# The small constant in the denominators of an attention block: added by ScalarE instead of by two matrix products of TensorE

## The chip, the cores and the metric

The kernel runs on one core of a Trainium2 chip. The metric is the device time of one execution in microseconds (us). A core has five engines that run their own instruction streams and wait for each other through semaphores: TensorE (PE in the profile, with PEld for its weight loads), VectorE (DVE), ScalarE (ACT), GpSimd (POOL) and SyncE (SP), which here only issues DMA transfers. Matrix products go into eight banks of PSUM; everything else lies in SBUF.

## The reference

Two blocks follow each other. The first is a kernelized attention over 4 batches, 4 heads, 1088 positions and head size 32. The second routes the 4352 rows that come out of it over 8 experts with Sinkhorn weights. Cut to what matters here:

```python
def phi(x):                       # 8 x 8 = 64 features of one position
    a = einsum('rd,bhsd->bhsr', S1, x)
    b = einsum('rd,bhsd->bhsr', S2, x)
    return einsum('bhsi,bhsj->bhsij', a, b).reshape(..., 64)

q_p, k_p = phi(q), phi(k)
kv  = einsum('bhsf,bhsd->bhfd', k_p, v)
z   = sum(k_p, axis=2)
num = einsum('bhsf,bhfd->bhsd', q_p, kv)
den = einsum('bhsf,bhf->bhs', q_p, z)[..., None] + 1e-06
x   = (num / den), turned to (4352, 128)

P = exp(x @ w_gate - max), then 8 times: rows normed, columns normed
out = sum over experts e of P[:, e] * (relu(x @ w1[e]) @ w2[e])
```

The change is about one term of it: the `+ 1e-06` in `den`, for batches 1 to 3.

## The kernel before

**Stages.** Nearly all TensorE work is the expert block: the two products per expert for chunks of columns of `xT`, the attention's result with the 128 features on the partitions. Expert work needs only the columns that are done, so the kernel does batch 0's attention first (`divide`, lines 398 to 413, which adds 1e-6 with a VectorE instruction of its own) and then mixes the attention of batches 1 to 3 with expert work on the columns that exist already. After that comes the routing (Sinkhorn), mixed with expert work too, and then the main part, `weighted()` (line 1111), in which VectorE and ScalarE run along with TensorE's 64 x 64 products (lines 1158 and 1311).

**Order of the work.** The order is written out by hand at lines 1578 to 1670. `attention(b)` (line 510) is a generator: it records one step of batch `b` and yields a number, and the caller records that much expert work with `fill(n)` (line 893). An expert block is a first product into a bank (`first`, L772, 64 output rows on each half of TensorE's columns), a Relu by ScalarE that copies it out (L774), differences on VectorE (L787) and, eight steps later, the second product (L836). TensorE and VectorE keep this order; ScalarE's instructions stand where they were recorded, and each engine runs its list strictly in order.

**Banks.** `bank()` hands out one of four PSUM banks (tile name `a`) for L772's results, for the key and query projections (L306, L429), for the key sums (L336) and for `tops`. A bank is free again when its last reader is done.

**Batches 1 to 3, step by step.** A batch is done in three parts `c` of 96 positions per quarter.

- `times(b, c)` (L456): VectorE makes the query features `ph`.
- `tops(b, c)` (lines 458 to 471): TensorE multiplies `ph` (as weights, 64 columns on each column half) with `kvs`, which holds `kv` and `z` side by side: 12 instructions with 66 columns (L465). They fill `pn`, a bank that reads as 3 x 4 x 33: 32 numerators and one denominator for each of 3 position groups and 4 heads. Then two more products (L469) with 12 columns add the constant: `ones` as weights, `eps` (a tile of 1e-6/128) as data, so that the sum over 128 rows is 1e-6, into the 12 denominator columns alone.
- `over(b, c)` (lines 475 to 484): VectorE takes the reciprocal of the 12 denominators out of the bank (L478), multiplies the numerators with it (L480) and turns the result (L484).
- `take_over` (line 486) brings the turned result through DRAM to `xT` (L489, L491): by GpSimd's queue, and for the last part of batch 3 by SyncE's. The routing's first product (`logits`, L499) reads it.

An instruction with fp32 operands shows in the trace as two TensorE records, so the 108 products of L465 are 216 records and the 18 of L469 are 36.

Of the kernel before, what the change touches and what calls it, by code (L numbers as in the profile page):

```python
# [11 lines left out]
F32 = mybir.dt.float32  # L12
U32 = mybir.dt.uint32
Act = mybir.ActivationFunctionType
# [38 lines left out]
def kernel(  # L53
# [12 lines left out]
    nc = tc.nc  # L66
    P = nc.NUM_PARTITIONS
    B, H, S, D = q.shape
# [14 lines left out]
    consts = ctx.enter_context(tc.tile_pool(name="consts", bufs=1))  # L83
# [11 lines left out]
    wk = early.enter_context(tc.tile_pool(name="wk", bufs=2))  # L95

    def bank():
        return aps.tile([P, 512], F32, tag="a", name="a")
# [14 lines left out]
    ones = consts.tile([P, P], F32, name="ones")  # L113
    nc.gpsimd.memset(ones, 1.0)
    warm = [aps.tile([P, 512], F32, tag="a", name="a") for _ in range(2)]
    for _ in range(6):
        for r in range(2):
            for c in range(2):
                rows, cols = slice(64 * r, 64 * (r + 1)), slice(64 * c, 64 * (c + 1))
                nc.tensor.matmul(warm[r][cols, 0:256], ones[rows, cols], ones[rows, 0:1].to_broadcast([64, 256]),  # L120
                                 start=True, stop=True, tile_position=(64 * r, 64 * c))
# [30 lines left out]
        kvs.append(consts.tile([P, 2, 2, D + 1], F32, name=f"kvs{i}"))  # L152
        nc.vector.memset(kvs[i], 0.0)

    eps = consts.tile([P, 3, H], F32, name="eps")
    nc.vector.memset(eps, 1e-6 / P)

    v_slots = []
    for i in range(2):
        t = wk.tile([P, H + 1, NT + 1, D], F32, name=f"v{i}", bufs=1)  # L160
# [123 lines left out]
    queries = {}  # L284
# [166 lines left out]
    def third(t, c):  # L451
        return t.rearrange("p i (s c n) -> p i s c n", s=2, c=3)[:, :, :, c]
# [5 lines left out]
    def tops(b, c):  # L458

        pn = bank()[:, 0:3 * H * (D + 1)].rearrange("p (t h d) -> p t h d", t=3, h=H)  # L460
        ph = third(phs[b % 2], c)
        for t in range(3):
            for i in range(2):
                for s in range(2):
                    nc.tensor.matmul(pn[64 * s:64 * (s + 1), t, 2 * i:2 * i + 2].rearrange("p h d -> p (h d)"),  # L465
                                     ph[:, i, s, 64 * t:64 * (t + 1)], kvs[b % 2][:, i].rearrange("p h d -> p (h d)"),
                                     start=(t == 0 and i == 0), stop=False, tile_position=(0, 64 * s))
        for s in range(2):
            nc.tensor.matmul(pn[64 * s:64 * (s + 1), :, :, D], ones[:, 0:64], eps, start=False, stop=True,  # L469
                             tile_position=(0, 64 * s))  # L470
        queries[b, c] = pn

    turned = {}

    def over(b, c):
        pn = queries.pop((b, c))
        rc = wk.tile([P, 16], F32, tag="rc", name="rc")[:, 0:12].rearrange("p (t h) -> p t h", h=H)
        nc.vector.reciprocal(rc, pn[:, :, :, D])  # L478
        xs = wk.tile([P, 512], F32, tag="rd", name="rd")[:, 0:384].rearrange("p (h t d) -> p h t d", h=H, t=3)
        nc.vector.tensor_tensor(xs.rearrange("p h t d -> p t h d"), pn[:, :, :, 0:D],  # L480
                                rc.unsqueeze(3).to_broadcast([P, 3, H, D]), op=Alu.mult)
        if c == 0:
            turned[b] = wk.tile([P, H, W9], F32, tag="xt", name="xt", bufs=1)
        nc.vector.transpose(out=turned[b][:, :, 96 * c:96 * (c + 1)].rearrange("p h (t s) -> p h t s", t=3), in_=xs)  # L484
# [25 lines left out]
    def attention(b):  # L510
# [6 lines left out]
        keys_kept(b)  # L517
        times(b, 1)
        tops(b, 0)
        if b == 1:  # L520
            transpose_q(2)
        yield 1.4
        if b == 1:
            over(b, 0)
            times(b, 2)
        else:
            times(b, 2)
            over(b, 0)
        tops(b, 1)
        if b == 1:  # L530
            queries_ab(2)
            repeat_a(2)
        if follows:
            repeat_b(b + 1)
        yield 1.4
        over(b, 1)
        if b + 1 == B:
            take_over(b, 0, 192, nc.gpsimd)
        yield 1.4
        tops(b, 2)  # L540
        if follows:
            transpose_k(b + 1)
# [1162 lines left out]
```

## Time and profile before

| | us |
|---|---|
| median of three runs | 883.63 |
| the three runs | 882.86 to 883.72 |
| the profiled execution | 883.02 |
| its span, first to last instruction | 881.2 |
| TensorE busy | 875.6 (99%) |
| VectorE busy | 724.0 (82%) |
| ScalarE busy | 384.6 (44%) |
| GpSimd busy | 262.8 (30%) |

The profile page gives busy time per engine, the span in 40 slices, the DMA queues, the chain of work that ended last, and groups of instructions by source line. Matrix products are pipelined, and their ends are modelled: what a product really takes of TensorE's time is read from the distance between starts, not from the duration shown. Further views of the trace that are used below: the timeline of a stretch (start, length, engine, line, operation, tiles, number of instructions, and in brackets the idle time before and what ended it), one source line's instructions with their waits, and the busy time by stage. The granted TensorE clock is full throughout.

### The profile page before, as it was taken

What the parts mean: (1) busy time and instruction counts of PE and PEld (TensorE: products, weight loads), DVE (VectorE), ACT (ScalarE), POOL (GpSimd) and SP (SyncE); (2) the same over time, 40 slices, a digit from 0 to 9 for tenths busy, and PEclk for the clock granted to TensorE, in tenths of its full rate; (3) what the DMA queues carried; (4) which work ended last, traced back from release to release, by engine and by line L of the source; (5) the groups of instructions that cost most, each with busy time, mean ns of one, the idle gap of its engine ahead of it and who ended that gap; (6) DMA issues with size and microseconds to landing.
All of it is one profiled execution on the core that took longest, in us unless ns stands there. A gap on an engine that the chain in (4) does not pass through costs nothing.

```text
span 881.2 us, 26159 instructions
## 1 busy us (share of the span) xinstructions
PE 875.6 (99%) x10828; PEld 572.4 (65%) x10828; DVE 724.0 (82%) x982; ACT 384.6 (44%) x792; POOL 262.8 (30%) x254
## 2 busy tenths in 40 slices
PE   9999999999999999999999999999999999999998
PEld 6788656877788655555555555555555566667876
DVE  8699689978888887778887778888788888888896
ACT  3455557644444433333343333334443344444442
POOL 3131125454433313222222222221323323312431
PEclk9999999999999999999999999999999999999999
DMA  8888399886666554444435544434755557567762
GB/s 260 270 273 264 96 233 245 130 260 195 197 195 198 171 160 128 136 144 128 129 94 144 137 125 126 117 115 109 194 152 148 154 139 216 152 152 220 219 194 49
DMA packets 120887, 149.08 MB, mean 169 GB/s; under 512 B 52288, under 2 KB 79808, under 8 KB 120384
## 3 DMA queue, kind: packets, MB, share of 16 engines
q1 hardware_dynamic: 112656, 136.92, 54.4%
q0 software_dynamic: 6720, 10.19, 5.8%
q8 instruction: 86, 1.41, 0.6%
q10 hardware_dynamic: 1392, 0.28, 0.2%
q14 instruction: 33, 0.27, 0.1%
HBM read 104.86 MB, written 25.99 MB: 148 GB/s over the span
## 4 chain that ended last, share of the span: by engine, by line
PE 99%; DMA 0%; DVE 0%; issue 0%; SPq 0%; DVEq 0%
PE pair L1158 39%; PE s L1311 39%; PE a L772 9%; PE s L836 7%; PE a L336 1%; PE a L465 1%; PE a L306 0%; DMA kx<-in_k_dram 0%; PE s L1323 0%; PE s L375 0%; PE a L429 0%; PE s L395 0%; PE a L499 0%; PE a L375 0%; PE a L395 0%; PE a L612 0%
## 5 line engine op out<-in xcount | busy, mean ns | idle before, releaser
L1158 PE MATMUL pair<-xf,w1x 64*64 64x320 f32 (+3 forms) x4496 | 574.1, 466 | 0.1
L1311 PE MATMUL s<-hb,w 64*64 64x480 f32 (+3 forms) x2544 | 363.4, 466 | 0.0
L1158 PEld LDWEIGHTS pair<-xf,w1x 64*64 64x64 f32 x4496 | 251.9, 133 | 116.7 <-issue 63.5
L1174 DVE CUSTOM_DVE_ANT_0 hb<-pair,copies 128x960 f32<-128x960 f32 (+3 forms) x234 | 214.8, 918 | 101.9 <-PE pair L1158 90.0
L1311 PE MATMUL s<-hb,ws 64*64 64x480 f32 (+3 forms) x1888 | 280.7, 468 | 0.0
L1311 PEld LDWEIGHTS s<-hb,w 64*64 64x64 f32 x2544 | 150.2, 133 | 76.3 <-issue 38.6
L1311 PEld LDWEIGHTS s<-hb,ws 64*64 64x64 f32 x1888 | 113.0, 133 | 56.6 <-issue 29.3
L1071 POOL TENSOR_TENSOR xf<-xT,pb 128x960 f32<-128x960 f32 (+3 forms) x40 | 70.3, 1759 | 241.0 <-ACT turn L1364 184.3
L1079 POOL TENSOR_TENSOR xf<-xf 128x960 f32<-128x960 f32 (+3 forms) x39 | 68.1, 1745 | 222.9 <-ACT turn L1364 141.1
L1171 ACT ACTIVATE hb<-pair 128x640 f32<-128x640 f32 (+3 forms) x86 | 66.4, 773 | 150.2 <-PE pair L1158 148.4
L772 PE MATMUL a<-xT,w 128*64 128x416 f32 (+3 forms) x512 | 123.0, 465 | 0.0
L774 ACT ACTIVATE hb<-a 128x416 f32<-128x416 f32 (+3 forms) x128 | 59.5, 468 | 65.7 <-PE a L772 60.5
L1216 DVE TENSOR_TENSOR hb<-hb 128x960 f32<-128x960 f32 (+3 forms) x78 | 74.8, 959 | 7.9 <-PE pair L1158 0.9
L1364 ACT COPY turn<-s 128x1 f32<-128x1 f32 x134 | 20.9, 156 | 137.5 <-PE s L1311 137.5
L1223 DVE TENSOR_TENSOR hb<-hb 128x960 f32<-128x960 f32 (+3 forms) x78 | 72.8, 933 | 7.4
L1219 DVE TENSOR_TENSOR hb<-hb 128x960 f32<-128x960 f32 (+3 forms) x78 | 75.0, 961 | 2.4 <-ACT hb L1171 0.6
L1252 ACT COPY copies<-pair 128x960 f32<-128x960 f32 (+3 forms) x78 | 59.9, 768 | 35.5 <-PE pair L1158 35.4
L1248 ACT COPY copies<-pair 128x960 f32<-128x960 f32 (+3 forms) x78 | 60.1, 770 | 33.0 <-PE pair L1158 33.0
L1243 ACT COPY copies<-pair 128x960 f32<-128x960 f32 (+3 forms) x78 | 59.9, 768 | 33.0 <-PE pair L1158 28.8
L1220 DVE TENSOR_TENSOR hb<-hb 128x960 f32<-128x960 f32 (+3 forms) x78 | 71.9, 922 | 0.0
L836 PE MATMUL s<-hb,ws 128*64 128x416 f32 (+3 forms) x224 | 71.6, 474 | 0.0
L787 DVE TENSOR_TENSOR hb<-hb 128x416 f32<-128x416 f32 (+7 forms) x84 | 56.8, 679 | 13.5 <-ACT hb L774 10.7
(207 smaller groups left out, 663.2 us busy)
## 6 DMA issues: line engine op xcount, KB each, us to landing
w1x<-w1x SPq DMA_DIRECT2D x87, 256.0 KB, 3.7
w<-w2x SPq DMA_DIRECT2D x71, 256.0 KB, 3.0
ws<-w2x SPq DMA_DIRECT2D x35, 256.0 KB, 3.5
pb<-pT SPq DMA_DIRECT2D x14, 480.0 KB, 4.2
xf<-xf SPq DMA_DIRECT2D x28, 240.0 KB, 3.5
w1x<-w1x SPq DMA_DIRECT2D x7, 896.0 KB, 5.9
ws<-w2x SPq DMA_DIRECT2D x36, 128.0 KB, 3.6
pb<-pT SPq DMA_DIRECT2D x13, 320.0 KB, 3.9
```

The costliest lines, as they stand in the source:

```text
L772: nc.tensor.matmul(ph[sl], loaded_w[j][0][:, P * f + H2 * s:P * f + H2 * (s + 1)], xT[:, at + lo:at + hi], start=True, stop=True, tile_pos ...
L836: nc.tensor.matmul(sums[g][i][H2 * s:H2 * (s + 1)], w, x, start=c == 1, stop=c == per, tile_position=(0, H2 * s))
L1071: nc.gpsimd.tensor_tensor(xf[:, 0:2].rearrange("p b n -> p (b n)"), xT[:, lo:lo + 2 * n], weights.pop(i), op=Alu.mult)
L1079: nc.gpsimd.tensor_tensor(xf[:, 4:6], xf[:, 1:4:2], xf[:, 0:2], op=Alu.subtract)
L1158: nc.tensor.matmul(out[H2 * col:H2 * (col + 1), r], w1[rows, PLACE[form], o:o + H2], xf[rows, x], start=start, stop=stop, tile_position=(H ...
L1171: nc.scalar.activation(out=x, in_=y, func=Act.Relu)
L1174: nc.vector._custom_dve(TENSOR_ADD_SAT, out=flat(out, n), in0=x, in1=flat(y, n), s0=math.inf, s1=0.0)
L1216: nc.vector.tensor_tensor(ts[0], h[3], h[0], op=Alu.subtract)
L1219: nc.vector.tensor_tensor(ts[1], h[3], h[1], op=Alu.subtract)
L1220: nc.vector.tensor_tensor(ts[2], h[1], ts[0], op=Alu.subtract)
L1223: nc.vector.tensor_tensor(ts[3], h[2], ts[2], op=Alu.subtract)
L1311: nc.tensor.matmul(out_[H2 * half:H2 * (half + 1)], w[rows], flat(x, n)[rows, r], start=c == 1, stop=True, tile_position=(H2 * rho, H2 * h ...
```

## The change

In `tops` the two products of `ones` with `eps` go; the last product of L465 now closes the accumulation. In their place one ScalarE instruction reads the 12 denominator columns from the bank, adds 1e-6 as a bias and writes them to the SBUF tile `rc`, which is now taken in `tops` instead of in `over`. `over` takes the reciprocal of `rc` in place and reads only the numerators from the bank. `eps` shrinks from 12 numbers per partition (1e-6/128 each) to one (1e-6). This happens nine times, three parts in each of batches 1 to 3.

```diff
-    eps = consts.tile([P, 3, H], F32, name="eps")
-    nc.vector.memset(eps, 1e-6 / P)
+    eps = consts.tile([P, 1], F32, name="eps")
+    nc.vector.memset(eps, 1e-6)
...
-                                     start=(t == 0 and i == 0), stop=False, tile_position=(0, 64 * s))
-        for s in range(2):
-            nc.tensor.matmul(pn[64 * s:64 * (s + 1), :, :, D], ones[:, 0:64], eps, start=False, stop=True,
-                             tile_position=(0, 64 * s))
-        queries[b, c] = pn
+                                     start=(t == 0 and i == 0), stop=(t == 2 and i == 1), tile_position=(0, 64 * s))
+        rc = wk.tile([P, 16], F32, tag="rc", name="rc")[:, 0:12].rearrange("p (t h) -> p t h", h=H)
+        nc.scalar.activation(out=rc, in_=pn[:, :, :, D], func=Act.Identity, bias=eps[:, 0:1])
+        queries[b, c] = pn, rc
...
     def over(b, c):
-        pn = queries.pop((b, c))
-        rc = wk.tile([P, 16], F32, tag="rc", name="rc")[:, 0:12].rearrange("p (t h) -> p t h", h=H)
-        nc.vector.reciprocal(rc, pn[:, :, :, D])
+        pn, rc = queries.pop((b, c))
+        nc.vector.reciprocal(rc, rc)
```

In the two built programs the lists of GpSimd and SyncE are the same; TensorE's list lacks the 18 products and is otherwise in the same order; ScalarE's has nine more instructions, each right behind the Relu of the expert block that stands before its `tops`.

## The prediction

> **What bounds the kernel.** I read the page's busy times first, then the chain that ended last, then the busy time of the stretch in which the nine changed places lie.
>
> ```profile
> span 881.2 us, 26159 instructions
> PE 875.6 (99%) x10828; PEld 572.4 (65%) x10828; DVE 724.0 (82%) x982; ACT 384.6 (44%) x792; POOL 262.8 (30%) x254
> PE 99%; DMA 0%; DVE 0%; issue 0%; SPq 0%; DVEq 0%
> 36.00:101.00 65.00, 65.00 (x854) 50.84 (x852) 56.26 (x95) 31.14 (x80) 13.40 (x23) 1.00 0.69 215
> ```
>
> The chain is TensorE from end to end, and between 36 and 101 us TensorE has no gap at all (65.00 of 65.00) at full clock (the 1.00), while ScalarE works 31.14 of them. So a slot that TensorE no longer spends moves the end, as long as nothing else makes it wait. What this stage is worth is read from starts, since the ends of products are modelled.
>
> **What the removed products cost.** First the line's instructions, then the first of the nine places on TensorE.
>
> ```profile
> L469 PEld LDWEIGHTS a<-eps,ones x36: 133/136/138, 37.6 to 99.8; 128*64 128x64 f32 x36
> L469 PE MATMUL a<-eps,ones x36: 176/192/206, 37.6 to 99.8; 128*64 128x12 f32 x36
> ...
> 36.91 0.87 PE L465 MATMUL a<-kvs,ph 128*64 128x66 f32 x24
> 37.61 0.24 PE L469 MATMUL a<-eps,ones 128*64 128x12 f32 x4
> 37.70 0.69 PE L772 MATMUL a<-xT,w 128*64 128x288 f32 x4
> 38.22 0.60 PE L836 MATMUL s<-hb,w 128*64 128x256 f32 x4
> 38.65 0.66 PE L772 MATMUL a<-xT,w 128*64 128x288 f32 x4
> 39.13 0.60 PE L836 MATMUL s<-hb,w 128*64 128x256 f32 x4
> ```
>
> The durations (176 to 206 ns, 36 records) would give 6.9 us, but they overlap. By starts the four records of a place hold the stream from 37.61 to 37.70, 0.09 us. The block behind them also starts slower: L772 to L836 is 37.70 to 38.22, 0.52 us, where the next block of the same shape takes 38.65 to 39.13, 0.48 us. Together 0.13 us. Would that 0.04 us stay, as the price of going from L465's narrow products to wide ones? Two other places tell.
>
> ```profile
> 30.99 0.70 PE L336 MATMUL a<-v,kp 128*64 128x64 f32 x18
> 31.52 0.60 PE L772 MATMUL a<-xT,w 128*64 128x256 f32 x4
> 31.95 0.60 PE L836 MATMUL s<-hb,w 128*64 128x256 f32 x4
> 32.38 0.39 PE L772 MATMUL a<-xT,w 128*64 128x256 f32 x2
> ...
> 122.74 0.92 PE L836 MATMUL s<-hb,w 128*64 128x416 f32 x4
> 123.44 0.29 PE L612 MATMUL a<-cs,ones 128*64 128x8 f32 x4
> 123.52 0.95 PE L772 MATMUL a<-xT,w 128*64 128x416 f32 x4
> 124.25 0.92 PE L836 MATMUL s<-hb,ws 128*64 128x416 f32 x4
> 124.95 0.51 PE L772 MATMUL a<-xT,w 128*64 128x416 f32 x1
> ```
>
> L336 has 64 columns, as narrow as L465, and the wide block behind it takes 31.52 to 31.95, 0.43 us, the same as the block after it (31.95 to 32.38). So the extra start belongs to the very narrow products and goes with them. L612 is nearly the same thing as L469 (`ones` as weights, 8 columns, four records): 123.44 to 123.52, 0.08 us, and 123.52 to 124.25, 0.73 us, against 0.70 us for the next block (124.25 to 124.95): 0.11 us. Between 0.11 and 0.13 us I take 0.12 us; nine places give 9 x 0.12 = 1.08 us. From below, 9 x 0.09 = 0.81 us, if only the slots between starts go; from above, 9 x 0.13 = 1.17 us.
>
> **What ScalarE adds.** Nine instructions of 128 x 12 from PSUM with a bias. None such is in the trace, so bounds from the nearest rows.
>
> ```profile
> L596 ACT ACTIVATE p<-kT,mx x1: 522/522/522, 119.3 to 119.3; 128x272 f32<-128x272 f32 x1
> L1364 ACT COPY turn<-s 128x1 f32<-128x1 f32 x134 | 20.9, 156 | 137.5 <-PE s L1311 137.5
> L270 ACT ACT_TABLE_LOAD x1 | 1.3, 1283 | 1.4 <-PEq L1689 1.4
> ...
> 38.50 0.41 ACT L774 ACTIVATE hb<-a 128x288 f32<-128x288 f32 x1 [1.33 <-PE a L772]
> 100.82 0.52 ACT L774 ACTIVATE hb<-a 128x416 f32<-128x416 f32 x1 [1.69 <-PE a L772]
> ```
>
> From below 0.156 us (the one-column copy out of PSUM), from above 0.522 us (the only instruction with a bias, 272 columns). Taking 260 columns off the latter at the slope of the Relus (0.41 us at 288, 0.52 at 416: 0.86 ns a column) leaves 0.30 us, which I take since the bias is the same. The Trainium skill, page "ScalarE: Activation LUTs", section "What ACT_TABLE_LOAD costs", gives 280 ns + 0.833 ns a column for an instruction with a pointer bias, an estimate of 0.29 us; by it the sum is the same, and no row of this trace has that size.
>
> Each new instruction stands in ScalarE's list behind the Relu of the block before, and waits for the last L465 product. What is queued behind it is the Relu of the next block, which TensorE's banks wait for. At the first place L465 ends about 37.78 us (36.91 + 0.87), so the new instruction runs to about 38.1, and the next Relu starts at 38.50 because it waits for its own product. The row at 100.82 shows the same pause behind the ninth place (1.69 us idle before its Relu). So ScalarE's 9 x 0.30 = 2.7 us lie in idle time; without that cover they would push Relus and with them the banks.
>
> **What changes on VectorE.** L478 now waits for ScalarE instead of TensorE, and behind it in VectorE's list stand L480, L484 and the differences that feed the second products.
>
> ```profile
>   PE a L469: 1.2, 1
> 39.14 0.23 DVE L478 RECIPROCAL rc<-a 128x12 f32<-128x12 f32 x1
> 50.26 0.56 DVE L480 TENSOR_TENSOR rd<-a,rc 128x384 f32<-128x384 f32 x1
> 51.67 0.41 PE L772 MATMUL a<-xT,w 128*64 128x288 f32 x1
> ...
> 99.75 0.23 PE L469 MATMUL a<-eps,ones 128*64 128x12 f32 x2
> 100.02 0.23 DVE L478 RECIPROCAL rc<-a 128x12 f32<-128x12 f32 x1 [1.22 <-PE a L469]
> 101.49 0.57 SPq L489 DMA_DIRECT2D xd<-xt  x1
> 105.28 1.76 SPq L491 DMA_DIRECT2D xT<-xd  x4
> DMA to landing us min/median/max: 1.7/1.8/1.9
> L499 PE MATMUL a<-xT,wg x4: 617/617/617, 109.0 to 109.1; 128*32 128x512 f32 x4
> ```
>
> VectorE waited at one place of nine (the row "1.2, 1"), the ninth; elsewhere it comes late by itself, as at 39.14, a microsecond after ScalarE would be done. The bank's release, the end of L480, does not move there either. The next writer stands closest at the third place: L480 ends at 50.82, and in the built order the L772 product that starts at 51.67 writes that bank next, 0.85 us later.
>
> At the ninth place the hop counts. L469's last record ends at 99.98 and L478 starts at 100.02. After the change the last L465 ends about 0.1 us earlier, but ScalarE stands between: 99.9 + 0.3 plus a wait makes L478 start near 100.3, 0.27 us later. Behind it hang L484, SyncE's L489 and the four L491 of the last columns of `xT`, then L499 on TensorE. The last L491 is issued about 106.6 and lands 1.7 to 1.9 us later, 108.3 to 108.5; L499 runs at 109.04: a cover of 0.5 to 0.7 us. It shrinks by 0.27 us and by the 0.12 us that TensorE gains here, to 0.15 to 0.35 us. Still hidden; if ScalarE took the upper 0.52 us, some 0.1 us would show.
>
> The reciprocal from SBUF and the smaller memset on VectorE lie off the chain; GpSimd's and SyncE's lists do not change, so no transfer is issued in another order.
>
> **The sum.** -1.08 us. The profiled execution took 883.02 us (its span plus 1.8), which gives 881.94; it lies 0.61 below the median of 883.63, from which the sum gives 882.55. The four known times have a mean of 883.31, so I take 882.2. That is -0.12%. About 0.2% (1.77 us) is what a measurement of this kernel can tell from no change.
>
> **Rivals.**
>
> Given back. The slots are saved, but TensorE waits for something that is timed by transfers: first of all L499 for `xT`, with a cover that I put at no more than 0.35 us. If ScalarE's hop were 1.4 us (0.35 + 1.08 over today's), all would be gone: 883.3. Against it: the largest bound is 0.52 us. For it: other covers later in the routing are not known to me.
>
> Slower or clearly faster by place in SBUF. In the built program every tile laid out after `eps` moves by 32 bytes, `hb`, `xT`, the weights and `xf` among them, so that nearly every TensorE operand starts at another offset.
>
> ```profile
> L1158 PE MATMUL pair<-xf,w1x 64*64 64x320 f32 (+3 forms) x4496 | 574.1, 466 | 0.1
> L1311 PE MATMUL s<-hb,w 64*64 64x480 f32 (+3 forms) x2544 | 363.4, 466 | 0.0
> L1311 PE MATMUL s<-hb,ws 64*64 64x480 f32 (+3 forms) x1888 | 280.7, 468 | 0.0
> ```
>
> These 8928 records run four at a time, 2232 slots. One nanosecond more in each is 2.2 us: it decides from (1.77 + 1.08) / 2232 = 1.3 ns up, and at 2 ns gives 883.31 - 1.08 + 4.5 = 886.7. With the other sign 0.3 ns are enough to pass 0.2%, and 1 ns gives 880.0. Against both: `ones`, which does not move and lies at a multiple of 64 bytes, and `ph`, which lies 32 bytes off one, load alike. The rows of L469 (136 ns in the middle) above and of L465 say so:
>
> ```profile
> L465 PEld LDWEIGHTS a<-kvs,ph x216: 132/137/139, 36.7 to 99.6; 128*64 128x64 f32 x108
> ```
>
> Slower by table loads. If Identity were not in the set that Relu, copies and Exp use, ScalarE would load twice at each place: 1.28 + 0.30 + 1.28 = 2.9 us where 0.7 us are free, so the next Relu comes 2.2 us late. TensorE has two more banks to go on with, 2 x 0.9 us at the first place (38.65 - 37.70), and then waits 0.3 us: nine times 0.3 us less the 1.08 us gives 884.9, more if the lateness adds up. It decides from a wait of 0.32 us a place (2.85 / 9). Against it: the trace has a single load, and so has the built list of the changed kernel. The Trainium skill's "ScalarE: Activation LUTs", section "Table sets: the hidden batching unit", says that cheap functions, identity among them, are filler in every set, and puts a switch at 2.66 us with its drain; the row of L270 has the same 1283 ns for the load.
>
> **How the numbers follow.** Forecast 0.70, given back 0.13, place in SBUF 0.05 slower and 0.09 faster, table loads 0.03. Of the forecast's 0.70 I count 0.11 as over 0.2% faster, since three times spread by 0.86 us and the forecast stands 0.7 us from that bound. So faster 0.11 + 0.09 = 0.20, same 0.59 + 0.13 = 0.72, slower 0.08. The likeliest case alone has 881.5 to 883.0 (sum 0.81 to 1.17 us, taken from 882.86 to 883.72 with some play). The range goes to 880.9 for part of the faster case and to 883.9 for the case of no gain.
>
> **What would show it.** Right: no L469 rows; L465 followed by L772 with the first block at 0.48 us; nine ScalarE rows of about 0.3 us; TensorE without gap from 36 to 101 us; L478 waiting once, for ScalarE; L499 without a wait; a shift of about 0.9 us of TensorE's events at the ninth place that stays to the end. Wrong: an idle row ahead of L499 or of a Relu, another table load, or changed distances between starts in the 480-column blocks.

## Result and profile after

The changed kernel takes 882.18 us (median of 22 runs, 881.43 to 883.31), the kernel before 883.39 us beside it (22 runs). The ratio is 0.9986 with a 95% interval of 0.9980 to 0.9991: 1.2 us faster, between 0.8 and 1.8 us. That is inside the 0.2% that were set as "no change that one measurement can tell"; with 22 runs on each side the interval excludes zero. The forecast was 882.2 us.

The page of the changed kernel, its span and engines:

```profile
span 880.1 us, 26108 instructions
PE 874.7 (99%) x10792; PEld 600.0 (68%) x10792; DVE 724.0 (82%) x982; ACT 386.8 (44%) x801; POOL 261.8 (30%) x254
```

The span is 1.1 us shorter. ScalarE has nine instructions more, TensorE 36 records less. (Lines behind 469 have numbers two lower than before: L770 is L772, L834 is L836, L497 is L499.) The first place on TensorE, from the timeline:

```profile
36.92 0.87 PE L465 MATMUL a<-kvs,ph 128*64 128x66 f32 x24
37.63 0.66 PE L770 MATMUL a<-xT,w 128*64 128x288 f32 x4
38.11 0.60 PE L834 MATMUL s<-hb,w 128*64 128x256 f32 x4
38.54 0.66 PE L770 MATMUL a<-xT,w 128*64 128x288 f32 x4
39.03 0.60 PE L834 MATMUL s<-hb,w 128*64 128x256 f32 x4
```

L770 follows L465 at once, and its first block takes 37.63 to 38.11, 0.48 us, where it took 0.52 us behind L469. The second one takes 0.49 us. Next ScalarE's new line and VectorE's reciprocal, each line's instructions with their waits, and the stretch with the nine places:

```profile
L469 ACT ACTIVATE rc<-a,eps x9: 270/270/271, 37.8 to 99.1; 128x12 f32<-128x12 f32 x9
  PE a L465: 6.4, 9
L476 DVE RECIPROCAL rc<-rc x9: 183/220/227, 40.1 to 99.4; 128x12 f32<-128x12 f32 x9
  ACT rc L469: 1.4, 1
36.00:101.00 65.00, 65.00 (x824) 50.61 (x822) 57.66 (x96) 33.81 (x89) 14.35 (x25) 1.00 0.72 223
```

ScalarE waits for L465 at all nine places (6.4 us in all) and then needs 270 ns. VectorE waits for ScalarE at one, the ninth. TensorE has no gap.

TensorE's stretch from the first to the last start of L465 holds eight of the nine places and nothing of the start of the kernel, whose first loads end up to a microsecond earlier or later from execution to execution. The row of L465 gives it, before and after:

```profile
L465 PE MATMUL a<-kvs,ph x216: 219/222/273, 36.9 to 99.7; 128*64 128x66 f32 x108
```

```profile
L465 PE MATMUL a<-kvs,ph x216: 219/222/272, 36.9 to 98.8; 128*64 128x66 f32 x108
```

62.8 us become 61.9 us, 0.9 us for eight places. Worked out from the starts of equal TensorE records in the two traces, the changed kernel gets ahead in steps: the distance does not change up to the first place, then it is -0.12 us, -0.19, -0.31, and behind the ninth -1.01 us. The steps are 0.116 to 0.118 us at eight places and 0.074 us at the second, and nothing over 5 ns comes between them. Behind the second place the products of L429 take 1.19 us in this execution; in `e4_change_without_move` below they take 1.15 us, and there all nine steps are 0.116 to 0.117 us, 1.05 us together. From 125 to 860 us the distance stays between -0.86 and -1.06 us.

### The profile page after: what moved, and what is told of

Its sections match the earlier page's. It is cut to its first block, busy times and chain, and to the rows that moved or that the text cites. A ratio compares the mean times of both kernels' runs of the same rounds, so it can differ in the third digit from the quotient of the medians.

```text
span 880.1 us, 26108 instructions
## 1 busy us (share of the span) xinstructions
PE 874.7 (99%) x10792; PEld 600.0 (68%) x10792; DVE 724.0 (82%) x982; ACT 386.8 (44%) x801; POOL 261.8 (30%) x254
## 4 chain that ended last, share of the span: by engine, by line
PE 99%; DMA 0%; DVE 0%; SPq 0%; issue 0%; DVEq 0%
PE pair L1156 39%; PE s L1309 39%; PE a L770 9%; PE s L834 7%; PE a L336 1%; PE a L465 1%; DMA kx<-in_k_dram 0%; PE a L306 0%; PE s L375 0%; PE a L429 0%; PE s L395 0%; PE a L497 0%; PE s L1321 0%; PE a L375 0%; PE a L395 0%; PE a L610 0%
## 5 line engine op out<-in xcount | busy, mean ns | idle before, releaser
L1156 PE MATMUL pair<-xf,w1x 64*64 64x320 f32 (+3 forms) x4496 | 552.1, 466 | 0.0
L1309 PE MATMUL s<-hb,w 64*64 64x480 f32 (+3 forms) x2544 | 354.2, 466 | 0.0
L1156 PEld LDWEIGHTS pair<-xf,w1x 64*64 64x64 f32 x4496 | 258.7, 133 | 110.3 <-ACT hb L1169 0.9
L1309 PE MATMUL s<-hb,ws 64*64 64x480 f32 (+3 forms) x1888 | 274.5, 468 | 0.0
L1309 PEld LDWEIGHTS s<-hb,w 64*64 64x64 f32 x2544 | 153.1, 133 | 63.4 <-ACT turn L1362 0.4
L1309 PEld LDWEIGHTS s<-hb,ws 64*64 64x64 f32 x1888 | 115.0, 133 | 47.2 <-DVE hb L1221 0.6
L770 PE MATMUL a<-xT,w 128*64 128x416 f32 (+3 forms) x512 | 122.7, 464 | 0.0
L772 ACT ACTIVATE hb<-a 128x416 f32<-128x416 f32 (+3 forms) x128 | 59.5, 468 | 57.1 <-PE a L770 51.7
L834 PE MATMUL s<-hb,ws 128*64 128x416 f32 (+3 forms) x224 | 71.6, 474 | 0.0
L770 PEld LDWEIGHTS a<-xT,w 128*64 128x64 f32 x512 | 54.5, 137 | 19.0 <-issue 7.2
```

The lines of the kernel that those rows point to most:

```text
L770: nc.tensor.matmul(ph[sl], loaded_w[j][0][:, P * f + H2 * s:P * f + H2 * (s + 1)], xT[:, at + lo:at + hi], start=True, stop=True, tile_pos ...
L834: nc.tensor.matmul(sums[g][i][H2 * s:H2 * (s + 1)], w, x, start=c == 1, stop=c == per, tile_position=(0, H2 * s))
L1156: nc.tensor.matmul(out[H2 * col:H2 * (col + 1), r], w1[rows, PLACE[form], o:o + H2], xf[rows, x], start=start, stop=stop, tile_position=(H ...
L1309: nc.tensor.matmul(out_[H2 * half:H2 * (half + 1)], w[rows], flat(x, n)[rows, r], start=c == 1, stop=True, tile_position=(H2 * rho, H2 * h ...
```

## Experiments

Each run is compared with the kernel before on the same chip in the same series. For each the L465 stretch is given, because the medians of 11 runs have intervals of about 0.8 us to either side, hardly finer than the effect, and the stretch has a tenth of a microsecond.

### The place in SBUF alone, and the change without it

`e2_move_alone`, against the kernel before:

```diff
-    eps = consts.tile([P, 3, H], F32, name="eps")
+    eps = consts.tile([P, 1], F32, name="eps")
...
-            nc.tensor.matmul(pn[64 * s:64 * (s + 1), :, :, D], ones[:, 0:64], eps, start=False, stop=True,
+            nc.tensor.matmul(pn[64 * s:64 * (s + 1), :, :, D], ones[:, 0:64], eps.to_broadcast([P, 3 * H]), start=False, stop=True,
```

> The kernel before with its products of ones and eps, but eps one column wide and read twelve times over, so that every tile behind it in SBUF moves by 32 bytes as in the changed kernel. If the 18 products are the whole of the change's gain: no change against before (0 +- 0.4 us), and TensorE's events stay where they are after each place. If part of the gain comes from the place in SBUF: faster by that part, up to 1.2 us, and spread over the 64 x 64 products instead of in steps at the nine places.

`e4_change_without_move`, against the changed kernel:

```diff
-    eps = consts.tile([P, 1], F32, name="eps")
+    eps = consts.tile([P, 12], F32, name="eps")
```

> The changed kernel with eps twelve columns wide, of which one is used: the change without the 32 bytes. If the place in SBUF does nothing: the changed kernel's time, 1.05 us under before. If it does: the difference to the changed kernel shows here with the other sign.

The move alone: 883.29 us, ratio 0.9995 (0.9987 to 1.0004). The change without it: 881.83 us, ratio 0.9979 (0.9970 to 0.9988). L465 in the first and in the second:

```profile
L465 PE MATMUL a<-kvs,ph x216: 219/222/272, 37.0 to 99.7; 128*64 128x66 f32 x108
```

```profile
L465 PE MATMUL a<-kvs,ph x216: 219/222/272, 37.0 to 98.8; 128*64 128x66 f32 x108
```

62.8 us by the exact starts, as before, and 61.8 us, as after to within the 0.04 us of the second place. In the main part (300 to 800 us) the move alone shifts equal TensorE records by 1 to 2 ns against before. The rival "place in SBUF" is out: the 32 bytes do nothing that the trace shows, and the gain is there without them.

### What a pair of products costs

`e3_products_twice`, against the kernel before (the constant halved):

```diff
-        for s in range(2):
-            nc.tensor.matmul(pn[...], ones[:, 0:64], eps, start=False, stop=True, ...)
+        for k in range(2):
+            for s in range(2):
+                nc.tensor.matmul(pn[...], ones[:, 0:64], eps, start=False, stop=(k == 1), ...)
```

> The kernel before with four products of half the constant at each place instead of two, so 18 more of 12 columns. If a product pair costs about 0.06 us of TensorE's stream each time and nothing hides it: slower than before by 36 more records, 1.05 us if the cost is linear; less, some 0.5 us (9 x 58 ns), if half of the measured 0.117 us a place is the passage from narrow to wide products, which is paid once. If the products lay in slack: no change.

884.48 us, ratio 1.0014 (1.0004 to 1.0023), 1.2 us slower. The first place in the timeline:

```profile
37.17 0.92 PE L465 MATMUL a<-kvs,ph 128*64 128x66 f32 x24
37.89 0.39 PE L470 MATMUL a<-eps,ones 128*64 128x12 f32 x8
38.10 0.71 PE L773 MATMUL a<-xT,w 128*64 128x288 f32 x4
38.61 0.63 PE L837 MATMUL s<-hb,w 128*64 128x256 f32 x4
39.04 0.68 PE L773 MATMUL a<-xT,w 128*64 128x288 f32 x4
39.53 0.63 PE L837 MATMUL s<-hb,w 128*64 128x256 f32 x4
```

Eight records hold the stream for 0.21 us where four held it for 0.09 us, so the second pair costs 0.12 us, and the block behind takes 0.51 against 0.49 us. The starts of equal records move by 0.116 to 0.118 us at each place. The second pair costs as much as the first, and nothing hides it.

`e7_products_66_columns` takes the version with VectorE adding the constant (below) and gives it two products of `ones` with zeros, 66 columns wide:

```diff
+    eps = consts.tile([P, 74], F32, name="eps")[:, 0:2 * (D + 1)]
+    nc.vector.memset(eps, 0.0)
...
+            nc.tensor.matmul(pn[64 * s:64 * (s + 1), 2, 2:4].rearrange("p h d -> p (h d)"), ones[:, 0:64], eps,
+                             start=False, stop=True, tile_position=(0, 64 * s))
```

> The version in which VectorE adds the constant, with two products of ones and a tile of zeros at each place, 66 columns wide where the kernel before has 12 (the result is the same). If a pair costs what its weight load takes, whatever its columns: TensorE's events shift by the same 0.117 us a place as with 12 columns. If the narrow products are the dear ones (the slow block behind them): 0.06 us a place or less. Against the version without any products: 1.05 us or 0.5 us slower.

883.51 us, ratio 1.0000 (0.9991 to 1.0008); the L465 stretch is 62.8 us (37.4 to 100.2), as with 12 columns, and TensorE's records keep the distances of the kernel before to within 6 ns over all nine places.

```profile
37.38 0.87 PE L465 MATMUL a<-kvs,ph 128*64 128x66 f32 x24
38.08 0.29 PE L469 MATMUL a<-eps,ones 128*64 128x66 f32 x4
38.20 0.66 PE L773 MATMUL a<-xT,w 128*64 128x288 f32 x4
38.68 0.60 PE L837 MATMUL s<-hb,w 128*64 128x256 f32 x4
39.11 0.66 PE L773 MATMUL a<-xT,w 128*64 128x288 f32 x4
```

With 66 columns the pair holds the stream for 0.12 us and the block behind it has its usual 0.48 us; with 12 columns it was 0.09 us and a block longer by 0.04 us. The sum is the same: the price is equal with 12 and with 66 columns. So it is 0.117 / 2 = 58 ns for each of the two passes of a pair (the records of the two column halves start 6 to 7 ns apart, so the halves work side by side). The products of L465 follow each other at the same distance: their 24 records start from 36.91 to 37.61 us in the kernel before, 0.70 / 12 = 58 ns. The Trainium skill, page "TensorE: Matmul & The Clock Gate", section "LDWEIGHTS (loading the stationary operand)", puts a weight load at its columns / 1.2 ns, which for 64 columns is an estimate of 53 ns; that a load of weights sets the 58 ns fits this, but no run here varies the weights' columns of so narrow a product. The records of the loads do grow with the columns in the kernel before (109 ns with 32 at L499, 137 with 64 at L465, 186 with 128 at L375), but they overlap the products, and what sets the 58 ns is not shown.

### ScalarE's hop without the saving

The hop is the way of the 12 denominators through ScalarE into SBUF. `e9_hop_alone`, against the kernel before, products kept:

```diff
+        rc = wk.tile([P, 16], F32, tag="rc", name="rc")[:, 0:12].rearrange("p (t h) -> p t h", h=H)
+        nc.scalar.copy(rc, pn[:, :, :, D])
-        queries[b, c] = pn
+        queries[b, c] = pn, rc
...
-        nc.vector.reciprocal(rc, pn[:, :, :, D])
+        nc.vector.reciprocal(rc, rc)
```

> The kernel before with its products, and in addition a ScalarE copy of the 12 denominators into SBUF, from which the reciprocal is taken: the hop without the saving. If ScalarE's instruction lies in idle time at all nine places: no change against before (0 +- 0.4 us), L478's successor waiting for ScalarE at the ninth place only. If the hop costs TensorE anything: slower by that, and the changed kernel's products would be worth more than 1.05 us.

883.22 us, ratio 0.9995 (0.9986 to 1.0004); the stretch is 62.8 us (37.2 to 100.0), as before. VectorE waits for ScalarE at one place. The hop is free here, with a copy of 168 ns; the next section has longer ones.

### A longer hop

`e5_hop_4` and `e6_hop_10`, against the changed kernel (ten in the second):

```diff
-        nc.scalar.activation(out=rc, in_=pn[:, :, :, D], func=Act.Identity, bias=eps[:, 0:1])
+        for _ in range(4):
+            nc.scalar.activation(out=rc, in_=pn[:, :, :, D], func=Act.Identity, bias=eps[:, 0:1])
```

> The changed kernel with the ScalarE instruction four times over at each place, so a hop of some 1.1 us instead of 0.27 us. The Relu behind it comes about 0.4 us late at each place, the reciprocal at the ninth place 0.8 us late. If the spare banks and the cover of the last transfers into xT hold: still about 1 us under before, no gap of TensorE from 36 to 101 us. If the cover at L499's place is the 0.15 to 0.35 us of the prediction: TensorE waits there some 0.5 us, and about half a microsecond of the gain stays.

> The same with ten in place of four: a hop of some 2.7 us, the Relu behind it 2.0 us late at each place, the ninth reciprocal 2.4 us late. The cover must be gone: TensorE waits for Relus at several places and for xT at the routing's first product; slower than before by 1 to 10 us. If it is not slower, ScalarE is not on any path here and the slack is larger than the idle times ahead of its Relus tell.

Four: 883.04 us, ratio 0.9994 (0.9985 to 1.0003). Ten: 886.88 us, ratio 1.0038 (1.0026 to 1.0051). With four the L465 stretch is 61.9 us (37.9 to 99.8), so the nine places cost nothing; 0.36 us are lost later, behind the routing's first products. The waits of TensorE in that run, and the busy time from 101 to 125 us:

```profile
PE a L771 <- DVE kT L507: 0.3, 1, 0.3
101.00:125.00 24.00, 23.71 (x155) 13.06 (x153) 17.96 (x33) 13.88 (x30) 1.84 (x4) 1.00 0.82 183
```

TensorE waits for a bank that VectorE's turning of the logits still reads. The changed kernel has no such wait. The reason lies in the built programs: which of the four banks `bank()` hands out follows from the scheduler's own idea of when they come free, and with the longer hop 4 of the 177 blocks that `bank()` hands out (the expectations below say 221), all around the logits, get another bank than in the changed kernel. The same is true of the version with VectorE (116 blocks), with ten (110) and with 66 columns (46), and of none of the others. So three kernels ran once more with the banks handed out in the changed kernel's order:

```diff
+    order = iter(...)   # the changed kernel's banks, one digit for each call
     def bank():
-        return aps.tile([P, 512], F32, tag="a", name="a")
+        return aps.tile([P, 512], F32, tag=f"a{next(order)}", name="a", bufs=1)
```

> The ScalarE instruction four times over again, with the four PSUM banks handed out in the order of the changed kernel (in the run before, 4 of the 221 blocks had another bank than there, all of them around the routing's first products). If the 0.36 us that TensorE lost there came from that order of banks: 1.05 us under before, no wait at L772 behind L499. If it came from the longer hop: again some 0.4 us under before, with a wait in that place.

> The ScalarE instruction ten times over, with the banks in the order of the changed kernel. The hop of 2.7 us is longer than any cover that the traces show, so it stays slower than before by 2 to 4 us, with waits of TensorE for Relus and late differences between 56 and 80 us and a wait for xT at the routing's first product of 1.5 to 2.5 us. If most of the loss goes with the other order of banks: within 1 us of before.

Four, `e10_hop_4_same_banks`: the wait is gone, and TensorE's records keep the changed kernel's distances from 42 to 150 us to within 5 ns (the stretch is 61.9 us).

```profile
101.00:125.00 24.00, 24.00 (x156) 13.30 (x154) 18.39 (x34) 14.21 (x30) 2.23 (x4) 1.00 0.85 188
```

The end of it is later all the same: 882.89 us, ratio 0.9995 (0.9986 to 1.0003). In its profile TensorE is 0.9 us late already at 30 us, before the first of the nine places, because VectorE's first transposition of the queries waited longer for their load (the changed kernel first, then this one):

```profile
14.70 1.31 DVE L289 STREAM_TRANSPOSE kT<-qx 128x1088 f32<-128x1088 f32 x1 [0.27 <-DMA qx<-in_q_dram]
```

```profile
15.66 1.31 DVE L294 STREAM_TRANSPOSE kT<-qx 128x1088 f32<-128x1088 f32 x1 [1.25 <-DMA qx<-in_q_dram]
```

So the same kernel ran again, on another chip:

> The run with ScalarE's instruction four times over and the changed kernel's banks, a second time. In its first profile TensorE was 0.92 us behind the kernel before already at 30 us, ahead of anything that was changed, and from there to 125 us it kept the changed kernel's steps exactly. If that delay at the start is chance of the execution: another delay at 30 us here, and the same steps behind it. If it belongs to this program: again 0.8 to 1.0 us at 30 us, and a median of some 0.4 us under before instead of 1 us.

882.56 us, ratio 0.9985 (0.9976 to 0.9994), and again 0.89 us late at 30 us in the profiled execution. `e5_hop_4` is 1.0 us late there as well, so all three profiles with four repeats start late; whether that belongs to the program stays open. The median of 0.4 us under before that was expected for that case did not come: it is 1.3 us under (0.0015 x 883.5). The same kernel, late in both profiles, gives two ratios that differ by 0.1%, so the profiled start does not tell the median, and a series of 11 runs repeats to about 0.1% only. What the trace says is the same in both: the eight places of the stretch gain their 0.9 us with a hop that is 0.8 us longer. At the routing's first product (about 109 us) TensorE loses 0.126 us against the changed kernel in this second profile, and nothing in the first: the cover there, the time between the landing of `xT` and the product that reads it, is about used up.

Ten, `e12_hop_10_same_banks`: 889.28 us, ratio 1.0063 (1.0050 to 1.0075), slower than the kernel before by 5.6 us (0.0063 x 883.3). Its L465 stretch is 65.5 us (36.9 to 102.4), 3.6 us more than in the changed kernel, and by the routing's first product at 109 us TensorE's records are 5.9 us later; from there the distance stays. That is more than I had expected. Of these 5.9 us, 1.3 come at that product (4.6 us at 106 us, 5.9 at 110). Three of TensorE's waits:

```profile
PE a L434 <- ACT rc L475: 1.0, 1, 1.0
PE a L776 <- DVE rd L484: 0.7, 2, 0.5
PE a L470 <- DVE rd L484: 0.5, 1, 0.5
```

L434 is the projection of the next batch's queries, L776 the expert block's first product, L470 the `tops` products (L429, L772, L465 of the kernel before): they wait for banks, the first for ScalarE's repeats themselves, the others for L484, VectorE's multiplication that reads the numerators last (L480 before). TensorE's weight loads wait for Relus as well, 2.1 us in four places. In the version with its own banks (`e6_hop_10`) the waits fall elsewhere, 0.7 us at 57 us, 0.4 at 70, 0.7 at 78, and 2.5 us at the routing, where `xT` now lands late:

```profile
112.69 0.59 PE L498 MATMUL a<-xT,wg 128*32 128x512 f32 x1 [1.54 <-DMA xT<-xd]
```

So both ways of "given back" exist, by the banks and by `xT`; between 0.8 us (three more instructions of 0.27 us) and 2.4 us (nine) of longer hop they begin to decide. The order in which banks are handed out sets where.

### The constant added by VectorE

`e8_add_on_vector` takes no engine in between: VectorE adds 1e-6 while it copies the denominators out of the bank, and ScalarE has nothing new. Against the kernel before:

```diff
-        for s in range(2):
-            nc.tensor.matmul(pn[64 * s:64 * (s + 1), :, :, D], ones[:, 0:64], eps, start=False, stop=True, ...)
...
-        nc.vector.reciprocal(rc, pn[:, :, :, D])
+        nc.vector.tensor_scalar_add(rc, pn[:, :, :, D], 1e-6)
+        nc.vector.reciprocal(rc, rc)
```

> Neither the products nor ScalarE: VectorE adds 1e-6 out of the bank into the SBUF tile and takes the reciprocal there, nine VectorE instructions of 128 x 12 more than before (about 0.2 us each), no hop to ScalarE. If all that counts is TensorE's stream: 1.05 us under before, as the changed kernel. If ScalarE's hop costs something in the changed kernel: more than 1.05 us under before. If VectorE is closer to the bound than its idle time tells: less.

882.59 us, ratio 0.9991 (0.9982 to 1.0000); the stretch is 62.1 us (37.0 to 99.1), 0.2 us more than with ScalarE. The waits of TensorE's weight loads between 55 and 60 us show one that the changed kernel does not have:

```profile
PEld s L834 <- DVE hb L785: 0.5, 1, 0.5
```

The second products wait for VectorE's differences, which begin at 55.99 us there and at 55.47 us in the kernel before. I took that for the price of nine more instructions on VectorE. But this is the version with 116 other banks, and so it ran again with the changed kernel's banks:

> The constant added by VectorE again, with the banks in the order of the changed kernel (116 of 221 blocks had another one in the run before). If the order of banks took 0.3 us of the gain: 1.05 us under before. If VectorE's nine additional instructions did, by making the differences (L787) late for the second products (L836): again 0.7 to 0.8 us under before, with TensorE late by some 0.25 us behind the third place.

882.66 us, ratio 0.9994 (0.9985 to 1.0003); its stretch is 61.9 us (37.6 to 99.5), as in the changed kernel, and TensorE's records keep the changed kernel's distances within 5 ns from 42 to 125 us. My reading fell: the 0.2 us came with the order of the banks, not with VectorE's added work. Much later, from 735 to 802 us, TensorE falls a further 0.27 us behind the changed kernel in `e7` and `e11` and 0.32 us in `e8`, the three in which VectorE adds, and in no other run more than 0.08 us. Weight loads wait for VectorE's differences there, 0.5 us at the longest where the changed kernel has 0.2; why, the runs do not show. Neither version is shown to be faster than the changed kernel.

## Why the prediction was right

- **The products' price**, 0.12 us a place by starts: 0.117 us measured, and 0.116 to 0.118 us for one more pair (`e3`). Going from overlapping durations (6.9 us) to distances between starts is what made the forecast; taken from the durations it would have been six times too large. That the 0.04 us of the slow block behind belong to the 12-column products holds: without them the block takes 0.48 us. `e7` refines it: with 66 columns the same 0.12 us lie wholly in the products, which I read so that the block behind pays what the products themselves do not fill of their pass; the trace does not show it directly.
- **ScalarE**, 0.30 us estimated: 0.270 us (row of L469). The Trainium skill, page "ScalarE: Activation LUTs", section "What ACT_TABLE_LOAD costs", makes it an estimate of 0.29 us, 7% above the row. Here the row decides. The plain copy of the same size in `e9` takes 102 ns less, 168 ns; it is another instruction, so that the bias alone makes the difference is not shown. Hidden, as forecast: `e9` has the hop without the saving and loses nothing, and `e10` and `e13` keep the steps at the nine places with a hop 0.8 us longer.
- **VectorE** waits for ScalarE at the ninth place alone, as forecast. L476 starts at 99.37 us, where L478 started at 100.02; TensorE is 0.88 us earlier there, so the reciprocal is 0.23 us late against TensorE (0.27 forecast).
- **The cover at the routing's first product** was mis-sized, without harm to the sum. It was to shrink to 0.15 to 0.35 us. SyncE's transfers in the changed kernel:

```profile
100.90 0.57 SPq L487 DMA_DIRECT2D xd<-xt  x1
103.87 1.76 SPq L489 DMA_DIRECT2D xT<-xd  x4
```

  From L487 to the first L489 are 2.97 us, where before they were 3.79 (101.49 to 105.28). That distance was carried over as fixed; over the profiles of this case it runs from 2.5 to 3.8 us, and the kernel before had the longest. The last L489 starts at 105.2 us and, with the 2.0 us to landing of the slowest transfer shown, is there at 107.2; L497 runs at 108.04: 0.8 us of cover. `e13` agrees with it: a hop longer by 0.81 us (three times 0.27) just uses it up and loses 0.13 us there, `e10`, the same kernel in another execution, nothing (the same sum leaves 0.0 us of cover in `e13` and 0.2 in `e10`). That those 0.13 us are the wait for `xT` is argued from this sum; the trace marks no wait.
- **The base** was taken as 883.31; 22 runs give 883.39. Less 1.08 that is 882.31, against 882.18 measured. That the forecast of 882.2 us meets the median to 0.02 us is luck: the gain is measured as 0.8 to 1.8 us, and the 1.15 us by which the profiled span is shorter hold 1.01 us from the nine places and about 0.15 us net from what comes later, above all the unexplained step at 866 us (below).
- **The shift at the ninth place** was to be about 0.9 us and to stay to the end. It is 1.01 us, and it stays to 860 us only: a further step follows at 866 us.
- **The rivals.** The place in SBUF is out (`e2`, `e4`). A table load is out: no further one is in the trace. "Given back" did not happen, but is real: `e6` and `e12` show it with a hop 2.4 us longer. I put the point at 1.4 us, from L497 alone; that the banks can give way as well I had only for the third place.

## What to carry to other kernels

Price a small matrix product by the distance between the starts of its neighbours, the block behind it included, and not by its duration or its columns: the pair here cost 0.117 us with 12 columns and with 66. The work that moved to an engine with idle time was free here as long as the hop stayed below the shortest cover behind it, so look for the place where a reader already waits (here one of nine). For an effect of 0.1%, compare distances within the traces between records that stand on either side of the change; medians of 11 runs hardly decide it, and a version whose PSUM banks are handed out in another order is not the same experiment.

## What was not expected

**A step at 866 us.** Besides the nine steps the trace shows one more, 0.30 us, near the end. VectorE reads the `pair` bank of the main part's last expert work (the kernel before first, then the changed one):

```profile
865.30 1.16 DVE L1174 CUSTOM_DVE_ANT_0 hb<-pair,copies 128x448 f32<-128x448 f32 x2 [0.62 <-PE pair L1158]
```

```profile
863.89 2.04 DVE L1172 CUSTOM_DVE_ANT_0 hb<-pair,copies 128x448 f32<-128x448 f32 x3 [0.27 <-PE pair L1156]
```

Before, and in `e2` and `e3`, it starts late, in all other versions it does not. Some of it is lost again by the end (span -1.15 us). Those other versions include `e9`, which gains nothing at the nine places, so the step does not follow the saving. Its cause is open.

**The start.** The wait for the query load was 0.27 us in the changed kernel's profile and 1.25 us in that of `e10`, a difference almost as large as the whole effect; that is why the stretch, and not the span, is compared here.

**The banks.** The choice of the bank is made when the program is built, and it moved in places that the change does not touch. 4 of 177 blocks with another bank cost 0.36 us in `e5`, 116 some 0.2 us in `e8`; the changed kernel itself has the banks of the kernel before.
